# Bringing the last rows of a first batch to the first MLP block: SBUF-to-SBUF transfers in place of direct products

## The chip, the core and the metric

The kernel runs on one core of one Trainium2 chip. The metric is device time in microseconds. The engines that appear below are PE (TensorE: matmuls, with PEld for its weight loads), DVE (VectorE), ACT (ScalarE), POOL (GpSimd) and SP (SyncE, which issues transfers). SP, ACT and POOL each have a queue of transfers; sixteen DMA engines carry them out. Numbers such as L625 are line numbers of the kernel before.

## What is computed

The reference is a Fourier mixing layer followed by an MLP with a hard-swish:

```python
X = np.fft.rfft(x, axis=1)                      # x: (8, 3008, 256)
Y = X * (filt_r + 1j * filt_i)[None, :, :]      # 1505 frequencies
y = np.fft.irfft(Y, n=3008, axis=1)
h = y.reshape(8 * 3008, 256) @ w_in             # w_in: (256, 2048)
g = h * np.clip(h + 3.0, 0.0, 6.0) / 6.0
out = g @ w_out                                 # w_out: (2048, 256)
```

All is float32.

## The kernel before, in words

**Transforms by factors.** The sequence length is 3008 = 47 x 64 (`NA`, `NC`). A forward transform over 47 (index `k`, of which 24, `KH`, are kept), a forward transform over 64 (`b_unit`, L549), the product with the filter (`f_unit`, three DVE instructions, L561 to L563), an inverse transform over 64 (`bi_unit`, L577; matmuls L584, copies out of PSUM L587) and an inverse over 47 (`n_first` for the first block, `n_five` and `n_unit` for the others) lead to token rows in `xn`. The 24 values of `k` are handled in pairs: unit `i` holds `k = 2i` and `2i + 1`, and `bi_unit(0, i)` takes two units, so four values of `k`. There are twelve units (`NU`), and six calls of `bi_unit` in batch 0, for `i` = 0, 2, ..., 10.

**From one inverse to the next.** The layouts of the two inverses differ: `bi_unit` leaves a tile `t` with the 64-point index on the partitions, and the inverse over 47 wants `k` on the partitions. For most data the crossing is made through device memory: `g_store` (L628, queue of POOL, L631) writes `t` to the array `g_tmp`, and loads bring it back to the tile `t4`. Tiles `t` alternate between the pool `t1p` (two buffers) and `t3p` (one buffer), so a copy at L587 can wait for an older store to have read its buffer.

**The first MLP block.** Block 0 needs 256 pairs of rows that come from six values (`FIRST`) of the 64-point index, `j` = 6 to 1, out of all 24 `k`. `n_first` (L735) makes them: 48 pairs of narrow matmuls (L765, `psn` and `po` from `t4` and the table `edges`), then six ACT copies to `xn` (L741, L744, L745). What `t4` must hold arrives in three ways:

- `k` = 0 to 11: four loads from `g_tmp` on SP (`first_load(0, 12)`, L663), after the stores of pairs 0, 2 and 4;
- `k` = 12 to 19: `g0_first` (L621) stores just the rows of pair 8 that block 0 needs, two transfers on ACT's queue and two on SP's (L625); then `first_load(12, 20)`, four loads on SP;
- `k` = 20 to 23: not through `t4` at all. `y_unit` (L566, two DVE instructions per unit) sums the filter products of units 10 and 11, and `direct` (L723) multiplies these by tables that hold both inverses at once (16 matmuls, L732), accumulating into the PSUM banks that `n_first` then goes on with. The tables, four pieces of 128 x 564 floats, are loaded by two transfers of SP (L1044, L1047).

**What follows.** The order of all work is written out by hand. After `direct`, `bi_unit(0, 10)` runs for the sake of the other blocks, then `n_first`, the two remaining stores `g_store(0, 8)` and `g_store(0, 10)`, and loads for batch 1 and for the weights. Meanwhile the weights are brought to the form that the MLP needs: `load_bits` has SP load a piece (L317), `w_abs` is two ACT instructions (L323, L324), `w_conv` and `w_conv_2` are six DVE instructions (L333 to L361), `w_sums` makes sums of weights on POOL (L369). `w_abs(1)` and `w_abs(2)` stand in ACT's order before the copies of `bi_unit(0, 10)`; `w_abs(3)` stands after `n_first`, and `convert(3)` on DVE (L1081) takes pieces 1, 2 and 3. Block 0 of the MLP is done with plain products (`plain_up`, `plain_down`), each step of it with further conversions in DVE's order; all later blocks use a scheme with fewer products that needs the sums of weights.

**Transfers and their completion counters.** In the built program every transfer of SP and ACT raises one of eight counters when it lands, and every transfer of POOL one of another eight. A transfer that reuses a counter is issued only once the one before it on that counter has landed; the issuing engine waits there, and everything behind it in its order waits too. The counters are handed out over SP and ACT together.

Of the kernel before, what the change touches and what calls it, by code (L numbers as in the profile page):

```python
# [10 lines left out]
FP32 = mybir.dt.float32  # L11
I32 = mybir.dt.int32
AXT = mybir.ActivationFunctionType
# [13 lines left out]
N = 3008  # L27
NA = 47
# [43 lines left out]
def late_row(j, h, a):  # L72

    if h == 0 or j == 0 or j > NJ or (j == NJ and a < SPLIT):
        return row(j, h, a)
    return (a - SPLIT if j == NJ else a) * NC + NC - j


def _make_tables():
# [73 lines left out]
    ones = np.zeros((P, 2, TOK))  # L153
    first = np.zeros((P, NJ + 1, TOK))
    last = np.zeros((P, NJ + 1, TOK))
    direct = np.zeros((P, TC, ND))
    for k in range(KH):
        for j in range(HC):
            for (ri, hh), x in terms(k, j, rows).items():
                if j in FIRST:  # L160
                    first[hh * 64 + ri * 32 + k, FIRST.index(j)] = first_of(x, FIRST.index(j))
# [9 lines left out]
        if k >= KH - TC:  # L171
            for q in range(64):
                fr = k + NA * q if q < 32 else NA * (q - 31) - k
                for n, j in enumerate(FIRST):
                    th = [2 * np.pi * ((fr * rows(j, h, a)) % N) / N for h in range(2)]
                    direct[q, k - KH + TC, n * TOK:(n + 1) * TOK] = 2 / N * first_of(np.cos(th), n)
                    direct[HALF + q, k - KH + TC, n * TOK:(n + 1) * TOK] = -2 / N * first_of(np.sin(th), n)
    wai = np.concatenate([t.reshape(P, -1) for t in (groups, ones, first, last)], axis=1)
    f = np.float32
    return wa.astype(f), wai.astype(f), wb.astype(f), wi.astype(f), wf.astype(f), start.astype(f), direct.astype(f)  # L180


@with_exitstack
def kernel(
# [8 lines left out]
):  # L193
    nc = tc.nc

    wa_np, wai_np, wb_np, wi_np, wf_np, start_np, direct_np = _make_tables()
# [6 lines left out]
    direct_d = nc.inline_tensor(direct_np, name="direct_t").ap()  # L203


    z_d = nc.dram_tensor("z_tmp", (B, KH, 2, HC, 2, D), FP32, kind="Internal").ap()
# [193 lines left out]
    def x0_at(o, n):  # L400
        return w_all.rearrange("p a b c m -> p (a b c m)")[:, ds(NP * 14 * P - HC * D + o, n)]
# [163 lines left out]

    def y_unit(b, i):  # L566
        s1, s2 = st["y", b, i]
        if b == 0 and i % 2 == 0:
            st["y0"] = t1p.tile([P, 2, 2, D], FP32, name="t1")
        y = yp.tile([P, 2, D], FP32, name="y") if b else st["y0"][:, i % 2, :, :]  # L570
        re, im = slice(0, HALF), slice(HALF, P)
        nc.vector.tensor_tensor(out=y[re], in0=s1[re], in1=s1[im], op=ALU.subtract)
        nc.vector.tensor_tensor(out=y[im], in0=s2[re], in1=s2[im], op=ALU.add)
        st["y", b, i] = y


    def bi_unit(b, i, ps=None):  # L577
        ys = [st.pop(("y", b, i + v)) for v in range(2)]
        ps = ps or [psF.tile([P, 2, D], FP32, name="psf", tag="f") for ri in range(2)]
        for v, ri in ((0, 0), (1, 0), (0, 1), (1, 1)):  # L580

            products = isinstance(ys[v], tuple)
            w, y = (wi[:, 1 + ri, :], ys[v][ri]) if products else (wi[ts(ri, 64), 0 if b else 3, :], ys[v][ts(ri, 64)])
            nc.tensor.matmul(ps[ri][ts(v, 64)], w, y, start=True, stop=True)  # L584
        t = t3p.tile([P, 3, 2, D], FP32, name="t3")[:, 0:2] if b or i & 2 else t1p.tile([P, 2, 2, D], FP32, name="t1")
        for ri in range(2):
            nc.scalar.activation(out=t[:, ri, :, :], in_=ps[ri], func=AXT.Copy)  # L587
        st["t3", b, i] = t

    def bi3_unit(b, i):  # L590
# [27 lines left out]
        for u in range(2):  # L618
            nc.gpsimd.dma_start(g_d[b, :, :, 2 * (i + 2) + u, :], t[ts(u, 64), 2])

    def g0_first(i):  # L621
        t = st["t3", 0, i]
        for v in range(2):
            for h in range(2):
                (nc.scalar, nc.sync)[v].dma_start(g_d[0, ds(h * HC + 1, NJ + 1), :, ds(2 * (i + v), 2), :].rearrange("c ri u d -> c ri (u d)"),  # L625
                                    t[ds(v * 64 + h * HC + 1, NJ + 1)].rearrange("p ri u d -> p ri (u d)"))

    def g_store(b, i):  # L628
        t = st.pop(("t3", b, i))
# [29 lines left out]
    def first_load(k0, k1):  # L659
        for h in range(2):  # L660
            for ri in range(2):
                p0 = h * 64 + ri * 32
                nc.sync.dma_start(t4[p0 + k0:p0 + k1, 0:NJ + 1, :],  # L663
                                  g_d[0, ds(h * HC + 1, NJ + 1), ri, k0:k1, :].rearrange("j k d -> k j d"))

# [54 lines left out]
            ready(i)  # L720


    def direct(i):  # L723
        if "psn" not in st:
            st["psn"] = {(c, dh): (psO.tile([P, 2, 2, P], FP32, name="po%d" % (2 + dh)).rearrange("p a u m -> p (a u m)")
                                   if c else psF.tile([P, 512], FP32, name="psn", tag="f"))
                         for c in range(2) for dh in range(2)}
        for u in range(2):
            k = 2 * i + u - KH + TC
            for (c, dh), ps in st["psn"].items():  # L730
                t, n = c * NJ * TOK, (1 if c else NJ) * TOK
                nc.tensor.matmul(ps[:, 0:n], st["y", 0, i][:, u, ts(dh, P)], st["direct"][k][:, ds(t, n)],  # L732
                                 start=k == 0, stop=False, skip_group_check=True)

    def n_first():  # L735
        for (c, dh), ps in st.pop("psn").items():
            for q, j in enumerate(chunks[c][1]):
                strips(ps[:, ts(q, TOK)], t4[:, j - 1, ts(dh, P)], edges[:, FIRST.index(j), :], start=False, stop=True)
# [24 lines left out]
    def strips(ps, w, x, **kw):  # L763
        for o in range(0, P, STRIP):
            nc.tensor.matmul(ps[ds(o, STRIP)], w[:, ds(o, STRIP)], x, skip_group_check=True, **kw)  # L765
# [214 lines left out]
    with tc.manual_schedule():  # L980
# [59 lines left out]
        nc.gpsimd.memset(t4, 0.0)  # L1040
        for c in range(FB, NT):
            table_load(0, c)
        last = x0_at(HC * D - 2048, 3 * ND)
        nc.sync.dma_start(last, direct_d[:, 0:3, :].rearrange("p k n -> p (k n)"))  # L1044
        load_bits(3)
        st["direct"] = [last[:, ts(k, ND)] for k in range(3)] + [st["rest"][:, 0:ND]]
        nc.sync.dma_start(st["direct"][3], direct_d[:, 3, :])  # L1047
        nc.sync.dma_start(edge, wai_d[:, ds(NW, ND)])
        load_bits(4)
        turn(0)  # L1050
        for c in range(NT):
            for i in (2 * c, 2 * c + 1):
                b_unit(0, i)
                f_unit(0, i)
                if c == NT - 1:
                    y_unit(0, i)
            if c + 1 < NT:
                turn(c + 1)
            if c:
                bi_unit(0, 2 * c - 2)  # L1060
                (g0_first if c == NT - 1 else lambda i: g_store(0, i))(2 * c - 2)
            if c == 4:
                first_load(0, KH - 3 * TC)
# [226 lines left out]
```

## Time and profile before

| what | value |
|---|---|
| three timed runs | 2608.02, 2608.52, 2608.97 us (median 2608.52) |
| span of the profiled execution, first to last instruction | 2607.0 us |
| PE busy in that span | 2591.8 us (99%) |
| DVE, ACT, POOL busy | 2053.9, 1295.6, 486.7 us |
| share of PE on the chain that ended last | 94% (DVE 3%, DMA 2%, POOL 1%) |
| `n_first`'s first matmul | at 61.62 us |
| first matmul of the later blocks' scheme | at 139.46 us |

The profiled execution has no time listed apart from its span; the span is 1.5 us under the median of the runs, and this difference is taken for what lies around it. The chain that ended last is followed back from the last instruction, at each step to what released it. Up to 139.46 us the chain goes over transfers, DVE and POOL in turn; from there on it is nearly all PE. So a microsecond more or less before 139 us is looked for in the start-up, stage by stage, and not in the engines' totals.

### The profile page before, as it was taken

To read this page: it belongs to the slowest core of one execution; us is meant where nothing else is said; L and a number is where in the kernel's file an instruction comes from. 1 tells how busy PE (TensorE), PEld (TensorE's weight loads), DVE (VectorE), ACT (ScalarE), POOL (GpSimd) and SP (SyncE) were. 2 spreads that over 40 slices of the span, in tenths; PEclk is the share of its full clock that TensorE was granted. 3 is DMA by queue.
4 is the path that set the end of the run, shared out by engine and by line. 5 is a ranking of instruction groups with operands and counts; after the bars stand their busy time and mean duration, and the time that the engine had idled before them with its cause. 6 is when DMAs were issued, how large, how long until landed. Compare 5 with 4: busy or idle time off the path is not lost.

```text
span 2607.0 us, 86613 instructions
## 1 busy us (share of the span) xinstructions
PE 2591.8 (99%) x37708; PEld 2051.0 (79%) x37708; DVE 2053.9 (79%) x3611; ACT 1295.6 (50%) x2677; POOL 486.7 (19%) x711
## 2 busy tenths in 40 slices
PE   8999999999999999999999999999999999999999
PEld 6487777878778787788877888777877778888887
DVE  7978868888788877888778887788877888766666
ACT  4554454545545455444554444545445454455554
POOL 2242021121211202111031210311113120111110
PEclk9999999999999999999999999999999999999999
DMA  8732234112241132411224112331123321110000
GB/s 247 224 92 81 59 101 119 54 33 87 74 123 54 33 87 78 119 54 37 83 83 114 54 38 82 89 108 54 54 66 91 106 57 49 50 44 24 20 22 26
DMA packets 130834, 200.32 MB, mean 77 GB/s; under 512 B 21602, under 2 KB 97472, under 8 KB 130262
## 3 DMA queue, kind: packets, MB, share of 16 engines
q1 hardware_dynamic: 115165, 150.12, 20.4%
q0 software_dynamic: 14720, 44.16, 6.1%
q8 instruction: 296, 4.85, 0.8%
q14 instruction: 84, 0.69, 0.1%
q10 hardware_dynamic: 569, 0.50, 0.1%
HBM read 122.43 MB, written 83.98 MB: 79 GB/s over the span
## 4 chain that ended last, share of the span: by engine, by line
PE 94%; DVE 3%; DMA 2%; POOL 1%; issue 0%; ACT 0%; SPq 0%; POOLq 0%; DVEq 0%; ACTq 0%
PE po L765 43%; PE al L765 24%; PE be L765 18%; PE psn L705 2%; PE psf L540 1%; PE psf L481 1%; PE psf L600 1%; PE be L600 1%; POOL w_all L369 1%; PE be L481 1%; DVE g L818 1%; DMA g_tmp<-t 1%; PE psf L765 0%; DMA ft<-in_filt_i_dram 0%; DVE y L335 0%
## 5 line engine op out<-in xcount | busy, mean ns | idle before, releaser
L765 PEld LDWEIGHTS po<-w_all,g 128*64 128x64 f32 x20808 | 1232.5, 137 | 247.0 <-issue 12.4
L765 PE MATMUL po<-w_all,g 128*64 128x128 f32 (+1 forms) x20808 | 1407.0, 274 | 1.4 <-DVE g L818 0.7
L813 ACT ACTIVATE r<-h,half_c 128x512 f32<-128x512 f32 x736 | 531.0, 722 | 346.7 <-DVE h L794 334.7
L765 PE MATMUL al<-xt,w_all 128*64 128x256 f32 x4416 | 664.0, 379 | 0.4 <-POOL w_all L369 0.3
L818 DVE SCALAR_TENSOR_TENSOR g<-r,h 128x512 f32<-128x512 f32 x736 | 536.2, 730 | 144.6 <-ACT r L813 129.2
L765 PE MATMUL be<-xt,w_all 128*64 128x256 f32 x2944 | 442.6, 379 | 0.0
L794 DVE TENSOR_TENSOR h<-be,s 128x512 f32<-128x512 f32 x368 | 253.8, 690 | 131.3 <-PE be L765 102.2
L760 POOL TENSOR_TENSOR xt<-xn 128x256 f32<-128x256 f32 x184 | 150.7, 838 | 890.3 <-ACT xn L687 890.3
L765 PEld LDWEIGHTS be<-xt,w_all 128*64 128x64 f32 x2944 | 211.3, 137 | 106.5
L765 PEld LDWEIGHTS al<-xt,w_all 128*64 128x64 f32 x4416 | 278.9, 137 | 1.7 <-POOL w_all L369 1.4
L808 ACT ACTIVATE h<-al 128x256 f32<-128x256 f32 x368 | 141.4, 384 | 273.2 <-PE al L765 272.4
L826 DVE TENSOR_TENSOR g<-g 128x512 f32<-128x512 f32 x367 | 261.4, 712 | 12.6
L799 DVE TENSOR_TENSOR h<-al,s 128x256 f32<-128x256 f32 x368 | 156.0, 424 | 135.6 <-PE al L765 130.5
L789 ACT ACTIVATE s<-al 128x256 f32<-128x256 f32 x368 | 141.6, 385 | 207.2 <-PE al L765 207.1
L765 PE MATMUL al<-xn,w_all 128*64 128x256 f32 (+1 forms) x1536 | 240.1, 393 | 1.1 <-DVE g L818 0.7
L765 PE MATMUL be<-xn,w_all 128*64 128x256 f32 (+1 forms) x1536 | 236.4, 388 | 0.0
L780 ACT ACTIVATE s<-be 128x256 f32<-128x256 f32 x368 | 141.4, 384 | 170.1 <-PE be L765 170.1
L825 DVE TENSOR_TENSOR g<-g 128x256 f32<-128x256 f32 x367 | 165.5, 451 | 12.6
L779 ACT ACTIVATE s<-al 128x256 f32<-128x256 f32 x368 | 141.5, 384 | 59.1 <-PE al L765 59.1
L831 DVE TENSOR_TENSOR g<-g 128x256 f32<-128x256 f32 x367 | 161.7, 441 | 2.4
L765 PEld LDWEIGHTS be<-xn,w_all 128*64 128x64 f32 x1536 | 110.3, 137 | 62.3 <-issue 7.4
L506 POOL DMA_DIRECT2D z_tmp<-t x144 | 72.0, 508 | 321.4 <-ACT s L780 296.0
(162 smaller groups left out, 1766.6 us busy)
## 6 DMA issues: line engine op xcount, KB each, us to landing
t<-g_tmp SPq DMA_DIRECT2D x184, 120.0 KB
t<-z_tmp SPq DMA_DIRECT2D x42, 512.0 KB
g_tmp<-t POOLq DMA_DIRECT2D x68, 256.0 KB, 4.3
z_tmp<-t POOLq DMA_DIRECT2D x120, 144.0 KB, 3.7
o_tmp<-o SPq DMA_DIRECT2D x46, 256.0 KB
xs<-in_x_dram SPq DMA_DIRECT2D x60, 192.0 KB
ft<-in_filt_r_dram SPq DMA_DIRECT2D x168, 64.0 KB
ft<-in_filt_i_dram SPq DMA_DIRECT2D x168, 64.0 KB
```

Source lines behind the costliest of these rows:

```text
L760: nc.gpsimd.tensor_tensor(out=o, in0=x0, in1=x1, op=op_)
L765: nc.tensor.matmul(ps[ds(o, STRIP)], w[:, ds(o, STRIP)], x, skip_group_check=True, **kw)
L779: nc.scalar.activation(out=s[:, 0, :], in_=al, func=AXT.Copy)
L780: nc.scalar.activation(out=s5, in_=be[:, 1, :], func=AXT.Copy)
L789: nc.scalar.activation(out=s[:, 1, :], in_=al, func=AXT.Copy)
L794: nc.vector.tensor_tensor(out=st["h"][0].rearrange("p (a n) -> p a n", a=2), in0=be, in1=s, op=ALU.add)
L799: nc.vector.tensor_tensor(out=st["h"][1][:, 256:512], in0=al, in1=s5, op=ALU.add)
L813: nc.scalar.activation(out=r, in_=st["h"][i], func=AXT.Relu, bias=half_c, scale=1.0 / 6.0)
L818: nc.vector.scalar_tensor_tensor(out=st["g", k, p][:, o:o + 2, :].rearrange("p a n -> p (a n)"), in0=st["r", i], scalar=1.0, in1=st["h"][i ...
L825: v.tensor_tensor(out=g[:, G1, :], in0=g[:, G3, :], in1=g[:, G22, :], op=ALU.add)
L826: v.tensor_tensor(out=g[:, G3:G2 + 1:2, :], in0=g[:, G3:G1 + 1, :], in1=g[:, G11:G11 + 1, :].broadcast_to([P, 2, 256]), op=ALU.subtract)
L831: nc.vector.tensor_tensor(out=g[:, G4, :], in0=g[:, G12, :], in1=g[:, G2, :], op=ALU.subtract)
```

## The change

The four `k` of pair 8 and the four of pair 10 (`k` = 16 to 23) go to `t4` straight from `t`, by transfers from SBUF to SBUF, one for each value of `k`, real or imaginary part and half: `first_rows`. Each moves six partitions of 1 KB to one partition of 6 KB. `direct`, its tables and their loads are gone, and so are `g0_first` and the `y_unit` calls of batch 0; `bi_unit(0, 10)` takes the filter products as the other pairs do, in another order of its four matmuls, and its second copy moves from ACT to DVE. `t4` has its rows in another order (`first_row`), so that `first_load` still covers consecutive partitions. Its second call brings `k` = 12 to 15 alone.

```diff
+def first_row(ri, k):
+    if k < KH - 2 * TC:
+        return ri * (KH - 2 * TC) + k
+    return 2 * (KH - 2 * TC) + (k - KH + 2 * TC) // 2 * 4 + 2 * ri + k % 2
...
     def bi_unit(b, i, ps=None):
-        for v, ri in ((0, 0), (1, 0), (0, 1), (1, 1)):
+        for v, ri in ((0, 0), (0, 1), (1, 0), (1, 1)) if i == NU - 2 else ((0, 0), (1, 0), (0, 1), (1, 1)):
...
         for ri in range(2):
-            nc.scalar.activation(out=t[:, ri, :, :], in_=ps[ri], func=AXT.Copy)
+            copy(ri and i == NU - 2, t[:, ri, :, :], ps[ri])
...
-    def g0_first(i):
-        t = st["t3", 0, i]
+    def first_rows(i, qs):
+        t, n = st["t3", 0, i], 0
         for v in range(2):
             for h in range(2):
-                (nc.scalar, nc.sync)[v].dma_start(g_d[0, ds(h * HC + 1, NJ + 1), :, ds(2 * (i + v), 2), :].rearrange("c ri u d -> c ri (u d)"),
-                                    t[ds(v * 64 + h * HC + 1, NJ + 1)].rearrange("p ri u d -> p ri (u d)"))
+                for ri in range(2):
+                    for u in range(2):
+                        r = h * 64 + first_row(ri, 2 * (i + v) + u)
+                        qs[n % len(qs)].dma_start(t4[r:r + 1, 0:NJ + 1, :], t[ds(v * 64 + h * HC + 1, NJ + 1), ri, u, :])
+                        n += 1
...
-        last = x0_at(HC * D - 2048, 3 * ND)
-        nc.sync.dma_start(last, direct_d[:, 0:3, :].rearrange("p k n -> p (k n)"))
         load_bits(3)
-        st["direct"] = [last[:, ts(k, ND)] for k in range(3)] + [st["rest"][:, 0:ND]]
-        nc.sync.dma_start(st["direct"][3], direct_d[:, 3, :])
...
                 f_unit(0, i)
-                if c == NT - 1:
-                    y_unit(0, i)
...
-                (g0_first if c == NT - 1 else lambda i: g_store(0, i))(2 * c - 2)
+                if c < NT - 1:
+                    g_store(0, 2 * c - 2)
             if c == 4:
                 first_load(0, KH - 3 * TC)
-        first_load(KH - 3 * TC, KH - TC)
+        first_rows(NU - 4, (nc.sync, nc.gpsimd))
+        first_load(KH - 3 * TC, KH - 2 * TC)
         for i in 1, 2:
             w_abs(i)
-        direct(NU - 2)
-        direct(NU - 1)
-
         bi_unit(0, NU - 2, [psU.tile([P, 512], FP32, name=n).rearrange("p (u d) -> p u d", u=2) for n in ("al", "be")])
+        first_rows(NU - 2, (nc.sync, nc.gpsimd, nc.scalar, nc.sync, nc.gpsimd, nc.scalar, nc.sync))
         load_bits(6)
```

`n_first` now opens its PSUM banks itself and starts them with `start=True`.

More of the change, by code (lines that the diff above doesn't have):

```diff
@@ L155, in _make_tables @@
     last = np.zeros((P, NJ + 1, TOK))
-    direct = np.zeros((P, TC, ND))
     for k in range(KH):
@@ L160, in _make_tables @@
                 if j in FIRST:
-                    first[hh * 64 + ri * 32 + k, FIRST.index(j)] = first_of(x, FIRST.index(j))
+                    first[hh * 64 + first_row(ri, k), FIRST.index(j)] = first_of(x, FIRST.index(j))
                 if j < 2:
@@ L170, in _make_tables @@
                     groups[hh * KH + k, j] = groups[HALF + hh * KH + k, j] = v
[L171 to L177, printed above, removed]
     wai = np.concatenate([t.reshape(P, -1) for t in (groups, ones, first, last)], axis=1)
     f = np.float32
-    return wa.astype(f), wai.astype(f), wb.astype(f), wi.astype(f), wf.astype(f), start.astype(f), direct.astype(f)
+    return wa.astype(f), wai.astype(f), wb.astype(f), wi.astype(f), wf.astype(f), start.astype(f)
 @with_exitstack
@@ L194 @@
     nc = tc.nc
-    wa_np, wai_np, wb_np, wi_np, wf_np, start_np, direct_np = _make_tables()
+    wa_np, wai_np, wb_np, wi_np, wf_np, start_np = _make_tables()
     wa_d = nc.inline_tensor(wa_np, name="wa_t").ap()
@@ L202 @@
     start_d = nc.inline_tensor(start_np, name="start_t").ap()
-    direct_d = nc.inline_tensor(direct_np, name="direct_t").ap()
     z_d = nc.dram_tensor("z_tmp", (B, KH, 2, HC, 2, D), FP32, kind="Internal").ap()
@@ L567, in y_unit @@
         s1, s2 = st["y", b, i]
-        if b == 0 and i % 2 == 0:
-            st["y0"] = t1p.tile([P, 2, 2, D], FP32, name="t1")
-        y = yp.tile([P, 2, D], FP32, name="y") if b else st["y0"][:, i % 2, :, :]
+        y = yp.tile([P, 2, D], FP32, name="y")
         re, im = slice(0, HALF), slice(HALF, P)
@@ L661, in first_load @@
             for ri in range(2):
-                p0 = h * 64 + ri * 32
+                p0 = h * 64 + first_row(ri, 0)
                 nc.sync.dma_start(t4[p0 + k0:p0 + k1, 0:NJ + 1, :],
@@ L720, in n_unit @@
             ready(i)
[L723 to L733, printed above, removed]
     def n_first():
-        for (c, dh), ps in st.pop("psn").items():
+        for c, dh in ((0, 0), (0, 1), (1, 0), (1, 1)):
+            ps = (psO.tile([P, 2, 2, P], FP32, name="po%d" % (2 + dh)).rearrange("p a u m -> p (a u m)")
+                  if c else psF.tile([P, 512], FP32, name="psn", tag="f"))
             for q, j in enumerate(chunks[c][1]):
-                strips(ps[:, ts(q, TOK)], t4[:, j - 1, ts(dh, P)], edges[:, FIRST.index(j), :], start=False, stop=True)
+                strips(ps[:, ts(q, TOK)], t4[:, j - 1, ts(dh, P)], edges[:, FIRST.index(j), :], start=True, stop=True)
             to = xn[:, dh, :, 0:PAIRS]
```

## The prediction

> **What bounds the kernel now.** I read the page's chain first: PE has 94% of it. Then the chain from 40 to 70 us, which holds the stage that the diff touches (columns: start, length, what).
>
> ```profile
> 49.87 0.37 ACT t L587
> 50.36 0.60 ACT t L587
> 50.98 4.56 DMA g_tmp<-t
> 55.56 2.31 DMA g_tmp<-t
> 57.88 0.26 SPq L663
> 58.19 3.34 DMA t<-g_tmp
> 61.62 1.86 PE psn L765 x40
> 64.22 1.94 PE al L765 x8
> 66.15 1.74 PE be L765 x8
> 68.64 0.69 DVE g L818
> ```
>
> The stage ends on transfers, not on PE: pair 8's tile is copied (to 50.96), ACT's first store lands at 55.54, only then does SP issue its second store (55.56), it lands at 57.87, the last load is issued at 58.19 and lands at 61.53, and `n_first` starts at 61.62. The 55.56 line is the thing to learn: SP did not lack data, which was ready at 50.96. Its store uses the completion counter of ACT's first store, so SP stood until that had landed. The direct products end at 59.8 and are hidden under this.
>
> Next, does a shift of `n_first` reach the end? I asked for the busy time of the stretches after it (length, then PE, PEld, DVE, ACT, POOL), and for DVE's order near 65 us.
>
> ```profile
> 68.70:121.00 52.30, 51.63 (x462) 25.09 (x462) 49.51 (x80) 28.40 (x47) 7.19 (x8) 1.00 0.76 228
> 121.00:139.50 18.50, 18.08 (x192) 11.41 (x189) 11.07 (x17) 9.31 (x21) 17.25 (x34) 1.00 0.58 157
> ```
>
> ```profile
> 63.60 0.43 DVE L337 TENSOR_SCALAR y<-y 128x512 int32<-128x512 int32 x1
> 65.64 0.69 DVE L354 TENSOR_TENSOR y<-g,y 128x512 f32<-128x512 f32 x1 [1.61 <-ACT g L324]
> ```
>
> From 68.7 to 121 us DVE is busy 49.51 of 52.30 us (conversions and hard-swish), then POOL 17.25 of 18.50 (sums of weights), then PE to the end. DVE enters late because `w_abs(3)` stands behind `n_first`'s copies on ACT. So each microsecond of `n_first` is a microsecond of the run, both ways.
>
> Last, prices of transfers on their issuing queue (minimum, median, maximum ns) and two readings of PE's clock.
>
> ```profile
> L625 ACTq DMA_DIRECT2D g_tmp<-t x2: 737/1038/1340, 51.0 to 52.4; - x2
> L625 SPq DMA_DIRECT2D g_tmp<-t x2: 721/824/928, 51.8 to 55.6; - x2
> L663 SPq DMA_DIRECT2D t<-g_tmp x8: 264/344/564, 49.9 to 58.2; - x8
> L957 SPq DMA_DIRECT2D out_dram<-o_tmp x18: 597/804/2022, 207.5 to 2564.5; - x18
> L421 PE MATMUL po<-p,w_all x10: 381/421/421, 6.6 to 8.5; 112*128 112x128 f32 x10
> L421 PE MATMUL po<-p,w_all x120: 275/275/421, 8.3 to 21.8; 112*128 112x128 f32 x120
> 2606.30:2607.00 0.70, 0.00 (x0) 0.00 (x0) 0.00 (x0) 0.00 (x0) 0.00 (x0) 0.50 0.00 0
> ```
>
> **The change part by part.**
>
> *Removed from PE and DVE.* 16 direct products (51.16 to 59.8 us, 8.6 us of PE) and four `y_unit` instructions of 0.69 us go; DVE gains one copy of some 0.7 us. Neither engine ends this stage. DVE's pieces 1 and 2 and the start of 3 then run inside the wait for `n_first`, and DVE still has to wait for `w_abs(3)`. Worth nothing, unless `n_first` came so early that DVE's 54.68 to 63.6 us of conversions became the end.
>
> *Removed loads.* 846 and 282 KB of tables leave SP's queue at 36.6 and 37.6 us. The store of pair 2 lands earlier than 47.02, so pair 6's copies (which waited 1.89 us) come about a microsecond sooner. Pair 8's second copy still waits for PE (its matmuls, 48.21 to 50.15) and ends at 50.96 as before. Worth nothing.
>
> *The last pair's tile.* DVE's filter products of unit 11 move from 51.09 up to 49.65 and end at 51.8; the last matmul ends near 52.5, DVE's copy at 53.2. On ACT `w_abs(1)` and `w_abs(2)` stand ahead; they took 53.15 to 55.52 and now follow the copies at 50.96, to 53.3. ACT's copy of 0.60 ends at 53.9. The one buffer of `t3p` must be released by the store of pair 6; that landed at 53.45 and comes earlier, so it is hidden.
>
> *The issue of the rows.* 32 transfers: 15 on SP, 13 on POOL, 4 on ACT. In the built program ACT's four, which carry the *last* pair, were given four of the eight counters ahead of most of SP's eight for pair 8. SP's third transfer reuses the counter of ACT's first, its fifth that of the second, its seventh that of the third, and the load behind them that of the fourth. So SP, with pair 8's data since 50.96, issues two rows and stands until ACT's first row has landed. All the rest is behind it on SP: six rows, four loads, the last pair's seven rows (the last three of these behind those loads' counters), then the loads of weights and of batch 1.
>
> What does one cost? No row of before moves SBUF to SBUF. Source and target shapes of these transfers differ (six partitions to one), as at L625 (six partitions to twelve pieces, 0.72 us on a quiet queue) and L957 (0.60 at least, 0.80 in the median); L663 has the same shape on both sides and takes 0.34. I take 0.74 plus 0.04 between issues, by L625, the nearest row; the ends are 0.34 and 0.93 (1.34 on ACT). Landing: L625's 2.31 us after the start of issue, in a quiet spell; the ends are 1.4 (the very last stores of the run, 2604.47 to 2605.87) and 4.56.
>
> The sum: ACT issues from 53.9, its first row lands at 56.2. SP's six rows, 6 x 0.78, to 60.9; four loads, 4 x 0.38, to 62.4; of the last seven the last is issued at 62.4 + 6 x 0.78 = 67.1 and lands at 69.4. The loads (issued from 60.9, landing in 3.3) release their counters in time. `n_first` starts near 69.4 instead of 61.62: 7.8 us later. At the cheap ends: ACT's row lands at 55.3, the load that the very last row waits for is issued near 58.4 and lands 2.83 later (56.44 to 59.27 before), the last row lands at 62.7: still 1.1 later. At the dear ends ACT's row lands at 58.5; six rows of 0.97, four loads of 0.6 and six more rows take it to 72.5, and landing in 4 makes 76.5: 14.9 later.
>
> POOL issues its 13 in about 0.55 each (L631's row: 0.55 to 0.77), the last near 58, and so is earlier than SP. The stores of pairs 8 and 10 follow there from 58 instead of 62.13; hidden. The loads behind SP (weights 4 and 5, issued at 58.54 before) slip by some 9 us, like everyone who uses them; hidden so long as `n_first` and the clock slip as much.
>
> *PE's clock.* Nothing is left for PE between 52.5 and 69.4 us. The trace shows the clock both ways: after the last matmul (ends 2601.7) the granted clock is 0.50 at 2606.3; at the start the first matmul runs at 3.02 and the same product takes 421 ns until 8.5 us and 275 after, at half the pace. So `n_first` meets a slow PE for about 5.7 us: its 2.1 us become 4.2, the copies take 0.5, and 1.0 us of the next products are at half pace: 2.1 + 0.5 = 2.6 us. The ends are 0 (clock kept) and 2.85 (half of 5.7).
>
> The Trainium skill ("TensorE: Matmul & The Clock Gate", Part 1) puts the idle window and the warm-up at about 3.4 us each. By its warm-up the loss would be half of 3.4, an estimate of 1.7 us in place of 2.6. Its rule speaks against this change, which trades hidden PE work for an idle PE.
>
> The sum, against the profiled execution: 7.8 + 2.6 = 10.4 us on a span of 2607.0, and 1.5 around it as in the runs: 2608.5 + 10.4 = 2618.9; I say 2618.5.
>
> The Trainium skill ("DMA: Bandwidth & Descriptors", Anatomy of one DMA) gives about 2.0 us as the fixed cost of a transfer, against L625's 2.31. With two landings in a row (ACT's first row, SP's last) the sum by it would be 0.6 us lower.
>
> **The rivals.**
>
> *Cheap transfers.* Issue costs 0.34, as at L663. For it: a row has six pieces only. Against it: L957 has hundreds of pieces and costs hardly more than L625, so the count is not what makes the price. `n_first` starts 1.1 to 3 later, plus 0 to 2.6 of clock: about 2612.
>
> *Dear transfers.* The queues are as busy as at 51 us (0.93 on SP, 1.34 on ACT, landing in 4). For it: POOL's stores fall into the same spell. Against it: the tables' 1.1 MB are gone. 14.9 + 2.6: up to 2626.
>
> *Faster.* SP's rows for pair 8 go out at 51 us because the counters do not hold them. Then at 0.34 each eight rows and four loads are issued by 55, the last seven from 55 to 57.5, and land by 59.2: 2.4 us early, 2606 if the clock holds. It decides once `n_first` starts before 61.6, less what the clock costs. Against it: the built program has these waits, and line 55.56 shows one of the same kind acting.
>
> *The delay is absorbed.* DVE's freed 2.1 us and the 2.8 idle us between 68.7 and 121 us take some of it up: 2616 to 2618. Against it: DVE's gaps there are hand-overs, and its freed time lies before the wait.
>
> **How the numbers follow.** 0.2% is 5.2 us, about what a measurement can tell from no change. Forecast, absorbed or not: 0.66, own range 2614 to 2622. Cheap: 0.16, mostly within 0.2%. Dear: 0.15. Faster: 0.03, and it would hardly reach 0.2%. So slower by over 0.2% is 0.84 (0.66, 0.15 and a little of cheap), within 0.2% is 0.14, faster is 0.02. The range leaves out about 1 in 10 on each side: from 2611.5, inside the cheap case, to 2624.5, inside the dear one.
>
> **What would show it.** On SP two row transfers near 51 us, then a gap to about 56 that ends when ACT's first row lands; rows of 0.7 us; `n_first` at 67 to 71 us; a granted clock under 1.00 around it and its `psn` matmuls at half pace; DVE idle for most of 63 to 73 us; from there the same work as before, shifted by an equal amount up to the end. Wrong: rows issued in 0.35 us, a clock that holds, or a shift at 139 us that is not that of `n_first`.

## The result, and the profile after

The changed kernel takes 2619.86 us (median of four runs, 2619.57 to 2620.67); the kernel before took 2608.27 us beside it (2608.00 to 2608.97). The ratio is 1.0045, with a 95% interval of 1.0033 to 1.0057: 11.6 us slower. The forecast was 2618.5 us in a range of 2611.5 to 2624.5.

The chain that ended last, in the changed kernel from 58 to 78 us (start, length, what), answers the first fence of the prediction:

```profile
58.27 0.61 POOL g_tmp L630
58.88 4.15 DMA g_tmp<-t
63.03 0.17 SPq L662
...
63.93 0.30 SPq L662
...
64.36 0.72 SPq L624
...
66.61 0.45 issue
67.06 0.69 SPq L624
...
68.55 0.69 SPq L624
...
69.28 1.87 DMA t<-t
71.16 0.35 issue
71.50 3.41 PE psn L754 x40
...
75.65 2.54 PE al L754 x8
```

The stage now ends on SP's row transfers, one behind the other at 0.69 us, and the landing of the last. `n_first` starts at 71.50 us where it started at 61.62, and its 40 `psn` matmuls take 3.41 us where they took 1.86.

Line numbers in views of the changed kernel and of the experiments are those of their own programs: L624 is the row transfers, L662 the loads of `first_load`, L630 the stores of `g_store`.

One step of this chain should not be taken at its word. The profile infers what released an instruction, and at 63.03 it names the landing of a store that POOL issued at 58.27. SP's loads there bring pair 6, and POOL issued pair 6's stores at 49.10; the store of 58.27 carries pair 8, which these loads don't read. Experiment 2 settles it: POOL's stores come later there (60.20), SP's loads sooner (56.72), and the chain has no step on POOL.

Why are SP's rows so late? SP's queue in order of time (start, length from first to last of the group, what):

```profile
51.21 10.99 SPq L624 DMA_DIRECT2D t<-t  x8
62.31 1.92 SPq L662 DMA_DIRECT2D t<-g_tmp  x4
64.36 5.61 SPq L624 DMA_DIRECT2D t<-t  x7
70.02 0.95 SPq L315 DMA_DIRECT2D xt<-in_moe_w_in_dram  x2
```

Eight rows of 0.69 us should take 5.9 us with their gaps, and they take 10.99. (One of them took 1.43 us.) What SP waited for between 50 and 64 us (waiter, released by, us in total, times, longest):

```profile
SPq L624 <- DMA t<-t: 3.3, 1, 3.3
SPq L624 <- DMA t<-g_tmp: 0.8, 1, 0.8
SPq L662 <- DMA g_tmp<-t: 0.8, 1, 0.8
SPq L624 <- ACT t L413: 0.6, 1, 0.6
```

The 3.3 us are SP's stand from 53.64 to 56.93. A row waits there for another row, although its own data, pair 8's tile, was there since 51.8. ACT issued its first row, one of the *last* pair, at 54.69 (1.29 us of issue), and it landed at 56.9. This is the wait that the prediction had read from the built program, and the recorded trace has the counter: SP's third row waits for number 108, which ACT's first row raises. The 0.8 us at SP's second row are a wait of the same kind, on the landing of a load.

The busy time of the stretches (length; PE, PEld, DVE, ACT, POOL; granted clock, DMA share, GB/s) shows the rest:

```profile
53.00:60.00 7.00, 0.82 (x2) 0.00 (x0) 5.77 (x10) 1.44 (x3) 7.00 (x14) 0.74 0.20 47
60.00:69.00 9.00, 0.00 (x0) 0.00 (x0) 3.61 (x7) 0.00 (x0) 0.72 (x2) 0.50 0.41 120
69.00:71.00 2.00, 0.00 (x0) 0.00 (x0) 0.00 (x0) 0.00 (x0) 0.00 (x0) 0.50 0.04 9
71.00:75.00 4.00, 3.50 (x45) 3.53 (x47) 0.00 (x0) 0.63 (x2) 0.00 (x0) 0.50 0.96 323
75.00:80.00 5.00, 4.88 (x26) 1.65 (x24) 2.67 (x4) 2.73 (x9) 0.00 (x0) 0.81 1.08 264
80.00:132.00 52.00, 50.83 (x456) 24.60 (x456) 49.01 (x79) 28.44 (x47) 6.79 (x7) 1.00 0.69 202
132.00:151.00 19.00, 18.86 (x194) 11.76 (x190) 11.39 (x17) 9.98 (x22) 17.14 (x33) 1.00 0.60 177
```

PE does nothing from 53.8 to 71.5 us, and from 56.4 the granted clock is 0.50; it is back at 1.00 at 76.9. The stretches from 80 on look as those from 68.7 did before, DVE 49 of 52 us, then POOL 17 of 19. DVE stood 13.18 us for `w_abs(3)`, which is behind `n_first`'s copies (DVE in order of time):

```profile
77.03 0.69 DVE L352 TENSOR_TENSOR y<-g,y 128x512 f32<-128x512 f32 x1 [13.18 <-ACT g L322]
```

**Where the 11.9 us between the two profiled spans lie.** The inverse of pair 8 starts at 48.21 us before and 49.14 after: 0.93 us. From there to `n_first` it is 13.41 us before and 22.36 after: 8.95 more. From `n_first` to the third hard-swish product on DVE (the third `g`) it is 13.05 before and 15.20 after: 2.15 more. Together 12.0, and the shift stays: 12.0 at the first product of `al` from `xt` (126.36 before, 138.35 after), 11.9 at the end. The 0.93 is not the change's. Batch 0's first inverse already starts at 30.42 before and 31.35 after, ahead of the place (36.6 us) where the first transfer that the change removes was issued; in the experiments it starts anywhere from 30.18 to 31.71, in variants of either kernel. The two differences, pair 8's inverse to `n_first` and `n_first` to the third `g`, are free of that start-up spread, so the experiments are read by them.

### The profile page after: what moved, and what is told of

Same layout as the page of the kernel before. It is cut to its first block, busy times and chain, and to the rows that moved or that the text cites. A ratio compares the mean times of both kernels' runs of the same rounds, so it can differ in the third digit from the quotient of the medians.

```text
span 2618.9 us, 86596 instructions
## 1 busy us (share of the span) xinstructions
PE 2587.8 (99%) x37676; PEld 2048.5 (78%) x37676; DVE 2051.2 (78%) x3608; ACT 1295.0 (49%) x2676; POOL 493.9 (19%) x724
## 4 chain that ended last, share of the span: by engine, by line
PE 97%; DVE 1%; DMA 1%; issue 0%; POOL 0%; SPq 0%; ACT 0%; POOLq 0%; DVEq 0%; ACTq 0%
PE po L754 44%; PE al L754 25%; PE be L754 18%; PE psn L704 2%; PE psf L538 1%; PE psf L479 1%; PE psf L596 1%; PE be L596 1%; PE be L479 1%; DMA w_all<-in_x_dram 0%; PE po L547 0%; PE psn L754 0%; PE psf L754 0%; PE psf L452 0%; PE psf L580 0%
```

## The experiments

The theory has three parts: SP's rows stand behind ACT's through shared completion counters; SP's rows cost 0.69 us each in a line; and the idle PE loses its clock. The rivals: the clock costs nothing because DVE and ACT set the pace anyway; row transfers land late whichever queue issues them; half of the rows would have been free.

### 1. Keep PE busy

The edit of the changed kernel, ahead of `n_first`:

```diff
+        psw = psF.tile([P, 512], FP32, name="psf", tag="f")
+        for i in range(36):
+            nc.tensor.matmul(psw, zero[:, P:2 * P], zero, start=True, stop=True)
         n_first()
```

> The changed kernel with 36 dummy matmuls (zeros, 128x512, a result that nobody reads) on PE between the last pair's inverse and the first block's rows; nothing else differs. Theory (the queue makes the first block late, the slow clock adds to it): the rows' first matmul starts as late as in the changed kernel (69 to 72 us), but runs at full pace; its 40 matmuls take 1.85 instead of 3.4 us and the time falls by 2.2 us to about 2617.6. Rival (the idle PE is the main cause): the time falls by 8 us or more, to 2612 or below. Rival (clock of no matter here): 2619.9 as before.

Measured: 2631.88 us (2630.62 to 2632.13), ratio 1.0092 (1.0077 to 1.0107). A miss, by a wrong size: each idle matmul shows as two records of 0.43 us, and the 72 records ended only at 85.2 us, long after the rows. PE in order of time:

```profile
54.12 31.17 PE L1059 MATMUL psf<-r 128*128 128x512 f32 x72
85.21 1.85 PE L754 MATMUL psn<-wai,t 128*64 128x94 f32 x40
```

Two readings survive. At full clock the `psn` matmuls take 1.85 us and the third `g` follows 13.05 us after `n_first`, exactly as in the kernel before, where the changed kernel has 15.20. And `n_first`, 23.59 us later than before, made the end 23.35 later: the shift carries in full.

### 2. No rows on ACT

Of pair 10's rows, ACT's four go to POOL.

```diff
-        first_rows(NU - 2, (nc.sync, nc.gpsimd, nc.scalar, nc.sync, nc.gpsimd, nc.scalar, nc.sync))
+        first_rows(NU - 2, (nc.sync, nc.gpsimd, nc.gpsimd, nc.sync, nc.gpsimd, nc.gpsimd, nc.sync))
```

> The changed kernel with the last pair's four row transfers of ACT given to POOL; SP keeps its 15, all shapes and the amount are the same. Theory (SP stands because ACT's transfers hold the completion counters that it reuses): SP issues pair 8's eight rows without the gap from 53.6 to 56.9 us, its last row near 64 to 65 instead of 69.3 us, the first block's rows start near 66 instead of 71.5, and the time falls by 4 to 6 us, to 2614 to 2616. Rival (the landing of SBUF-to-SBUF transfers, or POOL's slow issue, is what is late): POOL now has 17 rows and ends later, the rows start at 71 us or later, 2619.9 or more.

Measured: 2616.12 us (2615.41 to 2617.25), ratio 1.0032 (1.0021 to 1.0044). SP's queue:

```profile
50.51 6.10 SPq L624 DMA_DIRECT2D t<-t  x8
56.72 1.43 SPq L662 DMA_DIRECT2D t<-g_tmp  x4
58.27 6.62 SPq L624 DMA_DIRECT2D t<-t  x7
```

The first eight rows take 6.10 us and not 10.99, and `n_first` comes 18.46 us after pair 8's inverse and not 22.36. So ACT's rows, through the counters that ACT and SP share, cost 3.9 of the 8.95 us. POOL has 17 rows here and not 13, so the rival, POOL's slow issue or late landings, falls. The rest, 5.05 us, remains without ACT's rows.

### 3. Both

Experiment 2 with 22 idle matmuls.

> The two edits together (22 dummy matmuls, as the wait is shorter). Theory: the two parts add, 2612 to 2613.5; about 4 us over the kernel before remain, as SP still issues 15 rows of 0.7 us each one after the other. Rival (the clock loss only exists because the wait is long, so that the edits don't add): no more than 1 us under the run without ACT's transfers.

Measured: 2619.61 us (2619.54 to 2620.32), ratio 1.0046 (1.0030 to 1.0063). It has the wrong size of the first experiment: the idle matmuls ran from 53.31 to 72.4 us and held `n_first` at 72.39, 5 us after it could have started. The third `g` again follows 13.05 us after it.

### 4. Pair 8 alone by rows

The kernel before, with its direct products and tables, but pair 8's rows by `first_rows` on SP and POOL. Its edit of the kernel before, without the definitions of `first_row` and `first_rows`:

```diff
...
-                (g0_first if c == NT - 1 else lambda i: g_store(0, i))(2 * c - 2)
+                if c < NT - 1:
+                    g_store(0, 2 * c - 2)
...
-        first_load(KH - 3 * TC, KH - TC)
+        first_rows(NU - 4, (nc.sync, nc.gpsimd))
+        first_load(KH - 3 * TC, KH - 2 * TC)
```

> One part of the change alone: pair 8 reaches the first block by row transfers (eight on SP, eight on POOL), pair 10 by the direct products with their tables as in the kernel before. Theory: with ACT out of it SP issues its eight rows from 51 to 57 us and the loads to 58.5, the loads land near 61.5 to 62, PE is busy with direct products until 60 to 61 and stays warm; the rows start within 1 us of the kernel before, 2608 to 2609.5. Rival (each half of the transfers brings half of the loss, whatever stands around it): 2613 to 2615.

Measured: 2609.35 us (2608.75 to 2611.61), ratio 1.0006 (0.9997 to 1.0016): no difference that can be told. `n_first` comes 13.56 us after pair 8's inverse (before: 13.41), at full clock. Sixteen rows of pair 8 cost about what its four stores and loads cost, with none of them on ACT. So pair 8's rows alone lose nothing; the loss comes with the last pair's, which experiment 7 takes alone.

### 5. The clock, with the right size

The changed kernel with 19 idle matmuls at the place of experiment 1. (The 0.865 us of the expectation are from the rows of experiments 1 and 3, not of 2.)

> The changed kernel with 19 idle 128x512 matmuls between the last pair's inverse and n_first. By the second experiment's rows one takes 0.865 us (two passes of 0.43), so 19 take 16.4 us and end near 70.6, before the last row has landed (71.2). Theory (two losses: late rows, worth some 9.7 us, and a PE clock that has dropped, worth 2.2 us): the granted clock stays at 1.0, n_first starts at 71.5 to 72 as in the changed kernel, its 40 psn matmuls take 1.85 us and not 3.40, the third g product of the first block follows 13.0 us after and not 15.2, and the time is 2617.3 to 2618.0 (2.2 less than the changed kernel's 2619.9). Rival (the clock costs nothing, since DVE and ACT set the pace after n_first): the clock stays at 1.0 and the time stays at 2619.5 to 2620.

Measured: 2618.58 us (2617.36 to 2618.95), ratio 1.0039 (1.0025 to 1.0053). PE in order of time:

```profile
53.94 16.57 PE L1059 MATMUL psf<-r 128*128 128x512 f32 x38
71.74 1.84 PE L754 MATMUL psn<-wai,t 128*64 128x94 f32 x40 [1.22 <-DMA t<-t]
```

Here the idle matmuls end before the rows do, `n_first` is as late as in the changed kernel (22.42 us after pair 8's inverse, 22.36 there), the clock stays at 1.00, and the third `g` follows 13.04 us after it. The profiled spans, 2618.9 and 2616.7 us, differ by 2.2 us, with starts of the first inverse within 0.2 us; the medians differ by 1.3, less than expected, and the intervals of the two ratios overlap. So the 2.2 us are read from the stage of the trace; the times agree in sign and hardly settle the size.

### 6. The clock, without ACT's rows

Experiment 2 with 15 idle matmuls.

> The variant without rows on ACT's queue (2616.1) with 15 idle matmuls, 13.0 us, which end near 66.4, before its n_first (67.2). Theory: n_first at 67.2 to 67.7 at full pace, the time 1.6 less: 2614.2 to 2614.8. What is then left, some 6.5 us over the kernel before, is the issue of 15 rows on SP and the landing of the last. Rival (the clock costs nothing): 2616.

Measured: 2614.90 us (2613.87 to 2617.17), ratio 1.0027 (1.0018 to 1.0036). `n_first` comes 18.60 us after pair 8's inverse and the third `g` 13.04 after that, where experiment 2 had 18.46 and 14.59: 1.55 us of clock. By the medians it is 1.2.

### 7. The last pair alone by rows

Pair 8 by `g0_first` as before, pair 10 by rows on SP (7), POOL (5) and ACT (4), no direct products. Its edit of the changed kernel, without the new order of `t4`'s rows and the definition of `g0_first`:

```diff
...
-                if c < NT - 1:
-                    g_store(0, 2 * c - 2)
+                (g0_first if c == NT - 1 else lambda i: g_store(0, i))(2 * c - 2)
...
-        first_rows(NU - 4, (nc.sync, nc.gpsimd))
-        first_load(KH - 3 * TC, KH - 2 * TC)
+        first_load(KH - 3 * TC, KH - TC)
```

> Pair 8 by stores and loads as before, the last pair alone by rows (seven on SP, five on POOL, four on ACT); no direct products. Theory (SP's rows at 0.69 each in a line set the end, whichever pair they carry): SP's four loads of pair 8 go at 58, seven rows take it to 63.5, the last lands near 65.4, n_first at 65 to 66.5, the clock has dropped and costs 1.5 to 2.2; 2613 to 2615. Rival (only the rows of both pairs together are too many; one pair's go out beside the stores and cost nothing): n_first at 61.6 to 62.5, 2608 to 2609.

Measured: 2616.75 us (2615.74 to 2617.35), ratio 1.0032 (1.0020 to 1.0044). SP's queue:

```profile
51.25 3.70 SPq L621 DMA_DIRECT2D g_tmp<-t  x2
55.12 3.25 SPq L669 DMA_DIRECT2D t<-g_tmp  x4
58.48 5.18 SPq L631 DMA_DIRECT2D t<-t  x7
63.70 1.07 SPq L315 DMA_DIRECT2D xt<-in_moe_w_in_dram  x2
```

The rival falls: half of the rows is not free; `n_first` comes 19.23 us after pair 8's inverse. SP's rows ran to 63.66 us as expected, but `n_first` started at 67.77, later than the 65 to 66.5 of the theory. In the chain the last row, issued at 62.97, takes 3.99 us to land (1.87 in the changed kernel), and 0.81 more pass before PE starts; POOL's stores of 256 KB and SP's loads of 512 KB are under way there. The theory had no term for that. The third `g` follows 15.01 us after `n_first`, so the clock took 1.96 us.

### 8. Eight stores instead of four

The kernel before, with pair 8's four stores (on ACT's queue and SP's) as eight of half the size on SP and POOL, real and imaginary parts apart:

```diff
-                (nc.scalar, nc.sync)[v].dma_start(g_d[0, ds(h * HC + 1, NJ + 1), :, ds(2 * (i + v), 2), :].rearrange("c ri u d -> c ri (u d)"),
-                                    t[ds(v * 64 + h * HC + 1, NJ + 1)].rearrange("p ri u d -> p ri (u d)"))
+                    (nc.sync, nc.gpsimd)[n % 2].dma_start(g_d[0, ds(h * HC + 1, NJ + 1), ri, ds(2 * (i + v), 2), :].rearrange("c u d -> c (u d)"),
+                                        t[ds(v * 64 + h * HC + 1, NJ + 1), ri, :, :].rearrange("p u d -> p (u d)"))
```

> The kernel before with pair 8's four stores (two on ACT's queue, two on SP's, of 48 KB in 24 pieces) as eight of half the size on SP and POOL. Theory (what holds n_first in the kernel before is SP's second store, which stands until ACT's first store has landed): SP's stores go out at 51 to 54 us without a wait for ACT, the loads at 56 to 57, n_first at 60.6 to 61.2, where the direct products and the last pair's inverse take over as the bound; 2607.2 to 2607.8. Rival (the stores and loads take as long whichever queue issues them, or the direct products already end last): n_first at 61.6, 2608 to 2609.

Measured: 2608.26 us (2606.84 to 2611.24), ratio 1.0000 (0.9991 to 1.0009). The wait shown in the prediction at 55.56 us is gone: SP's four stores take 1.31 us from 52.00 on, its loads go at 55.59 to 57.16. The price of a store bears on the prediction (minimum, median, maximum ns of issue, first and last start):

```profile
L626 POOL DMA_DIRECT2D g_tmp<-t x4: 511/520/528, 50.8 to 52.4; - x4
L626 SPq DMA_DIRECT2D g_tmp<-t x4: 257/281/300, 52.0 to 53.0; - x4
```

`n_first` comes 12.54 us after pair 8's inverse, 0.87 sooner, and now follows the direct products and the last pair's inverse with no gap on PE. The time shows nothing of it: 0.87 us is 0.03%, and the interval reaches 0.09% to either side. (The expectation is wrong in one figure: the four stores are 24 KB in 12 pieces each.)

### 9. Take SP's last seven rows away

Experiment 2 without SP's rows of the last pair; those seven rows of `t4` stay at zero.

```diff
-        first_rows(NU - 2, (nc.sync, nc.gpsimd, nc.gpsimd, nc.sync, nc.gpsimd, nc.gpsimd, nc.sync))
+        first_rows(NU - 2, (None, nc.gpsimd, nc.gpsimd, None, nc.gpsimd, nc.gpsimd, None))
```

> The variant without rows on ACT's queue (2616.1, n_first 18.5 us after the start of pair 8's inverse) with SP's seven rows of the last pair left out: those seven rows of t4 stay at zero, and the first block is computed without them. Theory (after the counters and the clock, SP's row issue is what is left): SP ends with its four loads at 58.2, POOL issues its 17 rows to 60.1 and the last lands near 62; n_first 13.6 to 14.3 us after pair 8's inverse (62.3 to 63), 4.2 to 4.9 earlier; the clock has dropped and costs 1.5 to 2.2; time 2610 to 2611.5. Rival (the rows land late whichever queue issues them, because the DMA engines or POOL's queue are the limit): n_first stays 17 us or more after pair 8's inverse, 2615 to 2616.

Measured: 2614.25 us (2613.38 to 2615.21), ratio 1.0025 (1.0016 to 1.0034). Between the two forecasts, and nearer to the rival's: `n_first` comes 16.98 us after pair 8's inverse, 1.5 sooner than in experiment 2 instead of 4.2 to 4.9. POOL issued its rows as expected (50.3 to 59.4 us). But look at the row landings and at who else is on the DMA engines. POOL's row transfers in this kernel (the view lists landings for POOL's transfers alone):

```profile
L624 POOL DMA_DIRECT2D t<-t x17: 502/508/763, 50.3 to 58.9; - x17
DMA to landing us min/median/max: 1.6/1.7/5.8
```

and its windows (columns as above):

```profile
57.00:60.00 3.00, 0.00 (x0) 0.00 (x0) 2.79 (x6) 0.00 (x0) 3.00 (x7) 0.50 0.61 170
60.00:62.00 2.00, 0.00 (x0) 0.00 (x0) 1.93 (x4) 0.00 (x0) 1.79 (x4) 0.50 0.99 330
62.00:65.00 3.00, 0.05 (x2) 0.08 (x3) 0.68 (x2) 0.00 (x0) 0.00 (x0) 0.50 0.97 328
```

With its rows gone, SP went straight on to the loads of weights, 512 KB each, from 57.44 us. From 60 to 65 us the 16 DMA engines are busy for 97 to 99% of the time. POOL's rows issued up to 56 us landed in 1.6 to 1.9 us, those issued from 58 us on in 3.7 to 5.8. (The profile names a load of `xs`, batch 1's input, as what released `n_first` here. `n_first` doesn't read it; it landed at about the same time as the last row.) In the changed kernel these loads stand behind SP's own rows, and the DMA engines are nearly empty (share 0.04) when its last rows land.

### 10. The last inverse after `n_first`

Experiment 8 with `bi_unit(0, 10)` moved behind `n_first`.

> The eighth experiment's kernel (eight stores of half the size, n_first 12.5 us after the start of pair 8's inverse) with the last pair's inverse put after n_first on PE. Theory (the direct products and this inverse end last there): n_first 11.5 to 11.8 us after pair 8's inverse, the products of the first block begin 0 to 0.7 us earlier, since the inverse then stands between n_first and the first block; 2607 to 2608.2, not to be told from the kernel before. Rival (PSUM banks that the inverse and the first block share make the block wait for the copies out of them): the third g product of the first block follows 14 us or more after n_first, 2608.5 to 2610.

Measured: 2609.78 us (2609.08 to 2611.88), ratio 1.0009 (1.0000 to 1.0018). The rival's number: the third `g` follows 14.36 us after `n_first` and not 13.06. Its mechanism is only part of it: PE waits 0.73 us for an ACT copy of the inverse before the first product into `al`, but the chain to the third `g` goes over ACT, where the inverse's two copies now stand ahead of `w_abs(3)`. `n_first` gained nothing either (12.94 us), since in this execution the last load landed late; it waited 1.35 us for it with the direct products done.

### 11. Hold SP's large loads back

Experiment 9, with SP held after its four loads until `n_first`'s first copy, by a small transfer out of `xn`:

```diff
-        load_bits(6)
-        nc.sync.dma_start(wa[:, 0:528], wa_d[:, 0:528])
-        nc.sync.dma_start(wf, wf_d)
         n_first()
+        nc.sync.dma_start(wf[0:1, 0, 0:16], xn[0:1, 0, 0, 0:16])
+        load_bits(6)
+        nc.sync.dma_start(wa[:, 0:528], wa_d[:, 0:528])
+        nc.sync.dma_start(wf, wf_d)
```

> The ninth experiment's kernel, with SP held after its four loads until n_first's first copy is done (a 64-byte transfer out of xn into wf stands ahead of the loads of weights, tables and batch 1, which come after n_first). The same seven rows are left out. Theory (in the ninth experiment POOL's last rows landed 5.8 us after issue and not 1.7, because from 57.4 us SP's loads of 512 KB each shared the DMA engines with them): the last rows land in under 3 us, n_first 13.4 to 14.5 us after the start of pair 8's inverse, where the ninth had 17.0, the clock costs 1.5 to 2.2, time 2610.5 to 2612. Rival (rows on POOL's queue land late by themselves, or POOL's own stores behind them do it): n_first at 16.5 us or more after it, 2614 to 2615.

Measured: 2610.41 us (2610.24 to 2612.59), ratio 1.0010 (1.0001 to 1.0019). The landings of POOL's rows, and the window to set beside experiment 9's:

```profile
DMA to landing us min/median/max: 1.6/1.9/2.8
```

```profile
60.00:62.00 2.00, 0.47 (x6) 0.50 (x8) 1.90 (x5) 0.00 (x0) 2.00 (x4) 0.50 0.51 110
```

`n_first` comes 13.09 us after pair 8's inverse, 3.89 sooner than in experiment 9, and POOL's rows land in at most 2.8 us; POOL's issue is the same to 0.01 us, and POOL's stores still go right behind its rows. So it was SP's loads. And with 25 rows in place of 32, none of them in SP's second line and no load beside them, `n_first` is 0.32 us sooner than in the kernel before, while the clock takes 1.55 us (third `g` at 14.60).

### 12. The same hold in the kernel before

The edit of experiment 11 in the kernel before.

> The kernel before with the same hold on SP: no loads of 512 KB behind the last loads of pair 8. Theory (those loads share the DMA engines with the last four loads of t4, which landed 3.3 us after issue): they land in 2.2 to 2.6 us, n_first 12.6 to 12.9 us after the start of pair 8's inverse and not 13.4, 2607.0 to 2607.7, at the limit of what can be measured. Rival (3.3 us is what such a load of 24 KB takes in any company): n_first 13.4 us after it, 2607.6 to 2608.5.

Measured: 2609.51 us (2608.06 to 2612.92), ratio 1.0007 (0.9998 to 1.0016): a miss on the time. `n_first` comes 12.54 us after pair 8's inverse, 0.87 sooner, and is then bound by PE as in experiment 8 (so the landing itself was not told apart from other causes). But the third `g` follows 14.15 us after it. The chain shows why:

```profile
63.31 0.64 SPq L1072
63.95 0.06 issue
64.01 6.32 DMA xt<-in_moe_w_in_dram
70.33 0.02 issue
70.35 0.44 DVE y L333
```

The next pieces of weights, whose loads are issued at 58.5 us in the kernel before and at 64.0 here, land at 70.33 and DVE waits for it. What is off the path at 58.5 us is on it at 64.

## Why the prediction was right

**The wait on the counter.** Right, to a fraction of a microsecond. SP issued two rows, then stood; forecast until ACT's first row landed at 56.2, measured 56.9, of which 0.93 is the later start. Experiment 2 puts 3.9 us on it.

**The price of a row.** Right: 0.74 by the store of L625, measured 0.69 in the median on SP, 0.68 on ACT, and not the 0.34 of L663. POOL: 0.55 said, 0.51 measured. The row transfers of the changed kernel (columns as in experiment 8; the landings are those of POOL's 13):

```profile
L624 SPq DMA_DIRECT2D t<-t x15: 687/689/1427, 51.2 to 69.3; - x15
L624 POOL DMA_DIRECT2D t<-t x13: 502/511/734, 51.5 to 57.8; - x13
...
L624 ACTq DMA_DIRECT2D t<-t x4: 677/677/1285, 54.7 to 57.5; - x4
...
DMA to landing us min/median/max: 1.6/1.8/2.9
```

Experiment 8 comes near a test of the reason that the prediction gave, source and target of different shape. Its eight stores take the same tile from six partitions to six pieces of 2 KB, the same shape on both sides, and SP issued them in 0.26 to 0.30 us, where L625's, six partitions to twelve pieces, took 0.72 and 0.93. So the price of L625 goes with its form and not with the source in SBUF; nor is the count of pieces the reason, as L663 brings 48 or 72 and takes 0.34 and a row has 6 and takes 0.69. POOL's price didn't follow: 0.52 for these stores, 0.51 for a row. From SBUF to SBUF no other form was run, so for the rows themselves the reason stays an argument.

**The sum for `n_first`.** 7.8 us later was said; 8.95 it is, counted from pair 8's inverse. The terms that were mis-sized: of SP's six rows after the stand one took 1.43 us, so that they took 5.3 and not 4.7; the four loads took 1.92 and not 1.5; one of the last rows stood 0.45 for a counter; 0.35 passed between the last landing and PE's first matmul. Against these, the landing took 1.87 and not 2.31. SP's two slow issues, the row of 1.43 us and a load of 0.89, lie where POOL's four stores of 256 KB were on their way (from 58.27 us), and so does the slowest row of experiment 2 (1.32 us); no run separates the two.

The Trainium skill ("DMA: Bandwidth & Descriptors", Anatomy of one DMA) puts the fixed cost of a transfer at about 2 us, by a fit for transfers that POOL issues. POOL's rows agree: 1.8 us in the median. The prediction used the figure for rows of ACT and SP; they took 2.2 (ACT's first) and 1.87 (SP's last).

**Landing as a fixed time.** This step of the working was too simple, though it did no harm here. Experiments 9 and 11 show 5.8 or 2.8 us for the slowest of POOL's rows, by what else is on the DMA engines. In the changed kernel SP's late rows protect themselves, since the large loads stand behind them. Had the rows been as cheap as in the rival "cheap transfers", these loads would have come sooner and could have met the last rows on POOL; the prediction's 2612 for it had no term for this. That is an argument: no run had cheap rows.

**The clock.** Right in kind, between its two prices in size: 2.6 us said, 2.15 measured in the changed kernel (15.20 against 13.05, and 13.04 with PE kept busy in experiment 5). The term that was too large is `n_first` itself: up to the first product of `al` it took 4.15 us and not 2.60, so 1.55 more where 2.1 was said; its `psn` matmuls slowed by 1.8 and did not take twice as long. The products behind it lost 0.6, where 0.5 was said. The prediction read "half the pace" from a product of 421 and then 275 ns, which is a factor of 1.5.

That the warm-up of 5.7 us, read from the start of the run, came near the 5.4 measured is in part luck. Five kernels let the clock drop (times in us):

| kernel | PE idle | last matmul to the drop | clock at 0.50 for | `n_first`'s start to full clock | lost up to the third `g` |
|---|---|---|---|---|---|
| changed | 17.7 | 2.6 | 20.5 | 5.4 | 2.15 |
| experiment 7 | 14.5 | 2.5 | 17.1 | 5.0 | 1.96 |
| experiment 2 | 13.8 | 3.5 | 13.7 | 3.4 | 1.54 |
| experiment 9 | 12.3 | 4.0 | 13.7 | 5.4 | 2.12 |
| experiment 11 | 8.4 | 2.2 | 10.2 | 4.0 | 1.55 |

The fourth column is 6, 5, 4, 4 and 3 times 3.41 us. So in these traces the clock changes only at instants 3.41 us apart, and it rises at the end of the first such step that lies wholly behind `n_first`'s start. What is lost depends on where in a step `n_first` happens to begin, and not on how long PE was idle. The Trainium skill ("TensorE: Matmul & The Clock Gate", Part 1), with windows of about 3.4 us, gave 1.7: near experiments 2 and 11, short for the changed kernel, which began its work 2.0 us before the next step.

**One to one to the end.** Right: 12.0 us at the third `g`, 12.0 at 126 us, 11.9 at the end. The rival "the delay is absorbed" falls.

**Worth nothing.** The removed direct products did have a worth that the prediction booked under the clock: experiments 5 and 6 put idle matmuls in their place and get 2.2 and 1.55 us of the stage back. That the slipped loads cost nothing is right, but only because `n_first` slipped with them: in experiment 12 a load that slips by 5.5 us without `n_first` costs 1.1.

**The sum.** 10.4 us over the profiled execution was said, 11.1 it is by the two differences: 1.15 too little for the late start of `n_first`, 0.45 too much for the clock. That these partly cancel is luck. The prediction set 1.5 us between a span and its time; the changed kernel's runs list both, and there it is 1.8 (2618.9 and 2620.67).

**What stays open.** The medians of the variants lie 0.5 to 1.8 us above what the two differences give (experiment 8: 0.86 sooner in the stage, no gain in time). The profiled executions don't: with the start of the first inverse added, the two differences give every span to within 0.5 us. But the profiled execution of before, from which the differences are counted, was a long one: its span is 2607.0 us, and the executions beside the experiments have 2606.2 or less in the median. That is about 1 us of the gap; what made this execution longer was not found. No variant beat the kernel before.

## What to carry to other kernels

Look up which transfers share completion counters before moving one to another queue: a transfer whose data is ready can stand behind a later one's on a queue that it never touches. Count small transfers by their issue on one queue, at the price of the nearest row with the same kind of shapes, and count what stands behind them on that queue: once they leave, the large loads that follow come early and can slow the very rows that are waited for. Matmuls that look hidden under a transfer may be what holds PE's clock up for the critical work after it.

## What was not expected of the hardware

A row of 6 KB from SBUF to SBUF that POOL issued landed 1.6 to 2.9 us after issue in the changed kernel, in the median 1.8, and up to 5.8 us in experiment 9, where loads of 512 KB kept the DMA engines 97 to 99% busy. POOL issued such a row in 0.51 us, faster than SP (0.69) and ACT (0.68); but SP issued experiment 8's stores in 0.28 us and POOL took 0.52 for them. An idle matmul of float32 with 512 columns showed as two records of 0.43 us. And PE's clock came back 3.4 to 5.4 us after work began, by where the start fell between instants 3.41 us apart; the length of the idle time, 8.4 to 17.7 us, did not order the loss.
